# Two attention layers on one core: VectorE's exponential in five steps instead of seven, and eleven more tiles for it

## The chip, the core and the metric

The kernel runs on one core of one Trainium2 chip. The metric is the device time of one execution, in microseconds. Every run is listed with its time and with the mean clock that the profile shows as granted to TensorE, 1.000 being full speed. I call a run clean when its mean clock was 1.000. The experiments came in four sets, each on another chip with its own runs of the kernel before; the clean runs of that kernel have means of 1062.06 to 1062.43 us in the four sets, so comparisons across sets are good to some 0.4 us.

## The reference

Two equal layers over 2048 rows of 448, each an attention with 16 heads of 28 and an MLP with two gelus. Cut to what matters here:

```python
def _A_ref(x, wqkv, wo):
    qkv = (x @ wqkv).reshape(B, S, 3, H, Dh) ...          # S 2048, H 16, Dh 28
    scores = jnp.einsum("bhqd,bhkd->bhqk", q, k) * (Dh ** -0.5)
    p = _softmax(scores, axis=-1)                         # 16 x 2048 x 2048 exponentials per layer
    o = jnp.einsum("bhqk,bhkd->bhqd", p, v)
    return ... @ wo

x = A_x
x = x + _A_ref(_layernorm(x), A_wqkv, A_wo)
x = x + _B_ref(_layernorm(x), B_w1, B_w2, B_w3, B_w4)     # _B_ref: gelu(ln(x)@w1), shifts, @w2, gelu(ln@w3)@w4
x = x + _A_ref(_layernorm(x), A_wqkv, A_wo)
x = x + _B_ref(_layernorm(x), B_w1, B_w2, B_w3, B_w4)
```

## The kernel before

The 2 x 16 x 2048 x 2048 scores are 2048 tiles of 128x512. TensorE writes them into PSUM in 821 groups of alternately three and two tiles. ScalarE makes the exponentials of a group with one instruction. Some groups of three give their third tile to VectorE, where the program computes 2^x with integer arithmetic and a cubic in the fraction. `OFFL` says which groups these are.

```python
OFFL = ((48, 104, 6), (104, 150, 8), (150, 204, 6), (204, 300, 8), (500, 600, 8), (640, 731, 6))
EXPC = (0.30457565 * 128, 0.07826797 * 128)

def on_dve(n):                      # does group n give its third tile to VectorE?
    if len(grans[n]) < 3:
        return False
    ...
    return 1 <= grans[n][2][1] <= ... - 4 and any(a <= n < b and n % m == 0 for (a, b, m) in OFFL)

# VectorE's exponential (each yield op is one instruction; the buffer arguments are cut)
yield op("dve", ..., e.tensor_scalar(out=t32, in0=ps[:, bk, :], scalar1=0.0, scalar2=65536.0, op0=ALU.max, op1=ALU.mult))
yield op("dve", ..., e.tensor_scalar(out=fx, in0=lo, scalar1=2.0 ** -16, op0=ALU.mult))
yield op("dve", ..., e.tensor_scalar(out=ex, in0=fx, scalar1=EXPC[1], scalar2=EXPC[0], op0=ALU.mult, op1=ALU.add))
yield op("dve", ..., e.tensor_tensor(out=ex, in0=ex, in1=fx, op=ALU.mult))
yield op("dve", ..., e.tensor_scalar(out=fx, in0=fx, scalar1=-1.0, op0=ALU.add))
yield op("dve", ..., e.tensor_tensor(out=ex, in0=ex, in1=fx, op=ALU.mult))
yield op("dve", ..., e.scalar_tensor_tensor(out=PTD[:, slot, :], in0=t32, scalar=2.0 ** -9, in1=ex, op0=ALU.mult, op1=ALU.add))

# ScalarE's exponential of group n: cnt is 3, or 2 where VectorE has the third tile
yield op("act", e_dur(n), e.activation(out=PT[:, p0:p0 + cnt, :], in_=ps[:, b0:b0 + cnt, :], func=ACT.Exp, ...))
```

The order of all the instructions is not written by hand. When the program is built, a small scheduler plays the engines forward with estimated durations and picks what goes next. Where TensorE would wait, the scheduler adds a filler product of ones that nobody reads:

```python
SC.fill = (0.13, lambda e, b: e.matmul(out=ps[:, bi(b), 0:256], lhsT=ones_bf, rhs=ones_bf..., start=True, stop=True), ...)
```

The order was searched. `MOVES` holds two lists of (time, seed) pairs. At each time of the plan a random change, made from the seed, is applied to the latest starts by which the scheduler ranks its tasks. The lists are what a search over the scheduler's own estimate of the end has left:

```python
MOVES = [
    [(0.00, 453789), (24.05, 533123), (36.08, 574974), ...],      # 56 pairs
    [(0.00, 702263), (12.33, 381949), (24.47, 834893), ...],      # 56 pairs
]
plan = None
for k in range(ROUNDS):
    res = attempt(plan); plan = res[2].latest_starts(res[0])
for moves in MOVES[:-1]:
    res = attempt(plan, moves); plan = res[2].latest_starts(res[0])
est, P, SC = attempt(plan, MOVES[-1])
```

Of the kernel before, what the change touches and what calls it, by code (L numbers as in the profile page):

```python
# [8 lines left out]
ALU = mybir.AluOpType  # L9
# [487 lines left out]
def build_kernel(nc, A_x, A_wqkv, A_wo, B_x, B_w1, B_w2, B_w3, B_w4, out, n_layers=2):  # L497
# [11 lines left out]
    BIAS2 = 127.0  # L509
    WSH = 60.0 / LN2 + BIAS2  # L510
    DEFER = 4
    OFFL = ((48, 104, 6), (104, 150, 8), (150, 204, 6), (204, 300, 8), (500, 600, 8), (640, 731, 6))
    EXPC = (0.30457565 * 128, 0.07826797 * 128)
    TINY = 1e-20
    KCM = [(0, 112), (1, 112), (2, 112), (3, 112)]
    UBK = 5
    ROUNDS = 2
    MOVES = [
        [
            (0.00, 453789), (24.05, 533123), (36.08, 574974), (48.13, 374121), (60.22, 17501), (84.27, 918064), (96.41, 203548), (108.45, 909555),  # L520
            (120.45, 357456), (132.60, 615296), (168.83, 148562), (205.39, 389665), (229.56, 260273), (266.42, 71036), (278.44, 70253), (290.45, 97573),
            (314.58, 848798), (326.69, 359077), (338.81, 922778), (351.11, 731965), (364.52, 922857), (388.69, 388342), (400.73, 341387), (412.89, 278637),
            (425.04, 936161), (437.08, 80124), (449.22, 970104), (461.26, 151723), (473.36, 509392), (485.67, 278223), (497.71, 363728), (511.25, 320651),
            (523.31, 527451), (547.67, 931336), (572.39, 152194), (608.57, 394582), (620.75, 516554), (644.95, 174795), (669.10, 437522), (681.11, 304397),
            (693.35, 108309), (790.42, 21658), (838.85, 985952), (850.87, 674587), (862.89, 750586), (886.96, 618177), (929.37, 284043), (941.41, 596069),
            (953.46, 140073), (965.63, 696548), (977.66, 436165), (1001.89, 686219), (1014.11, 556019), (1026.13, 187601), (1038.16, 491035), (1050.33, 406353),
        ],
        [
            (0.00, 702263), (12.33, 381949), (24.47, 834893), (48.87, 33421), (61.01, 651789), (73.13, 100529), (85.19, 168019), (109.41, 146449),
            (146.15, 574177), (182.31, 891325), (194.40, 548019), (219.14, 396368), (231.29, 936970), (267.99, 701177), (280.01, 389568), (304.46, 941668),  # L530
            (316.78, 35337), (328.87, 201463), (353.05, 620046), (370.67, 421032), (382.82, 496206), (407.05, 974502), (419.21, 461357), (431.23, 484152),
            (443.42, 453671), (455.47, 313724), (479.69, 235889), (491.75, 227868), (516.71, 902926), (528.71, 143541), (540.72, 193750), (552.80, 710760),
            (576.97, 844584), (588.99, 232721), (601.11, 752264), (631.15, 288695), (643.22, 852623), (655.22, 951063), (679.25, 59294), (691.29, 109340),
            (703.74, 727887), (752.74, 761501), (777.12, 29398), (789.20, 616564), (801.25, 815928), (813.34, 33117), (837.60, 194148), (850.22, 728687),
            (890.63, 232155), (926.81, 41726), (939.16, 676561), (975.81, 264839), (987.86, 695881), (1003.27, 65585), (1027.57, 125777), (1039.58, 587050),
        ],
    ]
    GATE1 = ('qr', 0)
# [28 lines left out]
    def c_ps(n):  # L567
        return 0.07 + n * 0.00104

    def c_f2b(n):  # L570
        return 0.07 + n * 0.00052

    def c_b2b(n):
        return 0.07 + n * 0.00026
# [8 lines left out]
    with st:  # L583
        def sb(name, shape, dt):
            return st.enter_context(nc.sbuf_tensor(name, shape, dt))
# [6 lines left out]
        t32 = sb("t32", [128, 512], mybir.dt.int32)  # L592
# [15 lines left out]
        gt = sb("gt", [128, 512], FP32)  # L608
# [47 lines left out]
        def op(eng, dur, fn, reads=(), writes=(), **kw):  # L656
            return (eng, dur, fn, list(reads), list(writes), kw)
# [473 lines left out]
        def on_dve(n):  # L1131
            if len(grans[n]) < 3:
                return False
            L, u, g, p, kts, first, last = segs[grans[n][2][0]]
            return 1 <= grans[n][2][1] <= len(kts) * UNITS[L][u][1] // 4 - 4 and any(a <= n < b and n % m == 0 for (a, b, m) in OFFL)

# [15 lines left out]
        def pt_key(n, k):  # L1152
            return ("ptd", DVN[n]) if n in DVN and k == 2 else ("pt", n % 6)

        def t_dexp(n):
            bk, slot, at = gbank(n) + 2, DVN[n], DVL.index(n)
            yield ("acq", ["t32"])
            yield op("dve", 0.06 + c_ps(512), lambda e: e.tensor_scalar(out=t32[:, :], in0=ps[:, bk, :], scalar1=0.0, scalar2=65536.0, op0=ALU.max, op1=ALU.mult),  # L1158
                     reads=[("ps", bk)], writes=[("t32",)], last=[("ps", bk)])
            yield ("sig", ("d1", n))  # L1160
            for r in ("gt0", "gt1"):
                yield ("acq", [r])
            fx, ex = gt[:, 0:256].bitcast(FP16), gt[:, 256:512].bitcast(FP16)
            lo = t32[:, :].bitcast(mybir.dt.uint16).rearrange("p (n two) -> p n two", two=2)[:, :, 0]
            yield op("dve", c_f2b(512), lambda e: e.tensor_scalar(out=fx, in0=lo, scalar1=2.0 ** -16, scalar2=None, op0=ALU.mult), reads=[("t32",)], writes=[(("gt",), "gt0")])
            yield op("dve", c_b2b(512), lambda e: e.tensor_scalar(out=ex, in0=fx, scalar1=EXPC[1], scalar2=EXPC[0], op0=ALU.mult, op1=ALU.add),
                     reads=[(("gt",), "gt0")], writes=[(("gt",), "gt1")])
            yield op("dve", c_f2b(512), lambda e: e.tensor_tensor(out=ex, in0=ex, in1=fx, op=ALU.mult), reads=[(("gt",), "gt0"), (("gt",), "gt1")], writes=[(("gt",), "gt1")])
            yield op("dve", c_b2b(512), lambda e: e.tensor_scalar(out=fx, in0=fx, scalar1=-1.0, scalar2=None, op0=ALU.add), reads=[(("gt",), "gt0")], writes=[(("gt",), "gt0")])
            yield op("dve", c_f2b(512), lambda e: e.tensor_tensor(out=ex, in0=ex, in1=fx, op=ALU.mult), reads=[(("gt",), "gt0"), (("gt",), "gt1")], writes=[(("gt",), "gt1")])  # L1170
            if at >= 3:
                yield ("wait", ("pvd", DVL[at - 3]))
            yield op("dve", 0.06 + c_ps(512), lambda e: e.scalar_tensor_tensor(out=PTD[:, slot, :].bitcast(mybir.dt.uint16), in0=t32[:, :], scalar=2.0 ** -9, in1=ex, op0=ALU.mult, op1=ALU.add),
                     reads=[("t32",), (("gt",), "gt1")], writes=[pt_key(n, 2)])
            for r in ("gt0", "gt1", "t32"):
                yield ("rel", r)
            yield ("sig", ("d", n))

        def gbank(n):
            return 3 * (n % 2)  # L1180
# [35 lines left out]
        def t_attention():  # L1216
# [42 lines left out]
            for n in (0, 1):  # L1259
                if n in DVN:  # L1260
                    yield ("spawn", t_dexp(n), 1)
            for n in range(N):
                for (si, i, j) in grans[n]:
                    if i == 0 and j == 0:
                        yield ("sig", ("segstart", si))
                        if not segs[si][5]:
                            yield ("spawn", t_uload(si), 1)
                yield from pt_free(n)
                b0, p0, cnt = gbank(n), gblk(n), n_act(n)
                yield op("act", e_dur(n), lambda e, b0=b0, p0=p0, cnt=cnt: e.activation(out=PT[:, p0:p0 + cnt, :], in_=ps[:, b0:b0 + cnt, :], func=ACT.Exp, scale=LN2, bias=-BIAS2 * LN2),  # L1270
                         reads=[("ps", b0 + k) for k in range(cnt)], writes=[pt_key(n, 0)], tab="exp", main=n, last=[("ps", b0 + k) for k in range(cnt)])
                yield ("sig", ("e", n))
                if n + 2 < N:
                    yield from st_ops(n + 2)
                    if n + 2 in DVN:
                        yield ("spawn", t_dexp(n + 2), 1)
# [471 lines left out]
def bass_interleave_layers__mha_block__mixer_s_mlp__prompt_kernel(nc, A_x, A_wqkv, A_wo, B_x, B_w1, B_w2, B_w3, B_w4, out):  # L1748
    build_kernel(nc, A_x, A_wqkv, A_wo, B_x, B_w1, B_w2, B_w3, B_w4, out)
# [28 lines left out]
```

## Time and profile before

| | before |
|---|---|
| median of the first three runs | 1062.92 us (1061.68 to 1065.45) |
| its 42 runs beside the experiments | mean 1063.47 us, mean clock 0.9985 |
| 13 of these, the clean ones | mean 1062.24 us |
| profiled run | 1062.14 us, clock 1.0 |
| tiles on VectorE | 39 |
| ScalarE busy, TensorE busy, VectorE busy | 1022.6, 1022.5, 708.1 us |

How to read it: a page lists per engine its busy time and its share of the span, and then rows in which the span is cut into 40 slices with a digit for the busy tenths of each. The lines that bound the kernel are shown in the prediction below. One row of that page was left out there. It is TensorE's granted clock in tenths, slice by slice (a 9 is 90% or more):

```profile
PEclk9999999999999999999999999999999999999999
```

In the profiled run the clock never fell (1.00 in all stretches).

### The profile page before, as it was taken

The page shows a single profiled execution, that of the slowest core. Times are in us where ns is not written, and L with a number is a line of the kernel's source. Part 1 is how long each engine was busy: PE and PEld are TensorE (multiplying, and loading weights), DVE is VectorE, ACT ScalarE, POOL GpSimd, SP SyncE. Part 2 cuts the span into 40 slices and gives each one's busy share as a digit, 9 for nine tenths or more (in the row PEclk, how much of TensorE's full clock was granted, in tenths as well). Part 3 has the DMA queues.
Part 4 walks back from the last instruction along what each step waited for, and adds up shares of the span by engine and source line. Part 5 has one row for each costly group of instructions (what it writes and reads, how often), then busy time and mean ns, then how long its engine had stood idle before and what let it go on. Part 6 is the DMA issues. An engine that isn't in the chain of part 4 may idle for free.

```text
span 1060.3 us, 20859 instructions
## 1 busy us (share of the span) xinstructions
PE 1022.5 (96%) x8896; PEld 397.1 (37%) x8912; DVE 708.1 (67%) x1707; ACT 1022.6 (96%) x939; POOL 56.9 (5%) x78
## 2 busy tenths in 40 slices
PE   8999999999999999999999999999999999999998
PEld 5233333333333333334333443333333333444446
DVE  7977678775877647863489426657777966377544
ACT  6999999999999999999999999999999999999984
POOL 2000000000001001010010000000010100010000
PEclk9999999999999999999999999999999999999999
DMA  4232140000010001100020002211120001010000
GB/s 116 81 108 83 36 121 21 16 1 21 3 19 21 1 1 40 36 21 1 1 61 31 27 11 61 70 32 48 32 45 1 2 21 35 23 25 2 1 19 23
DMA packets 70709, 35.01 MB, mean 33 GB/s; under 512 B 56472, under 2 KB 65048, under 8 KB 70616
## 3 DMA queue, kind: packets, MB, share of 16 engines
q1 hardware_dynamic: 70616, 33.68, 11.9%
q8 instruction: 69, 1.13, 0.4%
q14 instruction: 24, 0.20, 0.1%
HBM read 12.70 MB, written 7.08 MB: 19 GB/s over the span
## 4 chain that ended last, share of the span: by engine, by line
ACT 60%; PE 34%; DVE 4%; DMA 1%; issue 1%; POOL 0%; SPq 0%; POOLq 0%; DVEq 0%
ACT PT L1270 53%; PE ps L661 9%; PE ps L1244 9%; PE ps L1319 8%; PE ps L1687 5%; ACT h2T L1651 4%; PE ps L664 3%; ACT L1651 1%; ACT gt L1434 1%; ACT L1270 1%; DMA h2T<-in_A_wqkv_dram 1%; DVE hT L1407 1%; DVE qT L969 0%; DMA uscr<-uin 0%; DVE gw L1420 0%
## 5 line engine op out<-in xcount | busy, mean ns | idle before, releaser
L1270 ACT ACTIVATE PT<-ps 128x1024 bf16<-128x1024 f32 (+1 forms) x821 | 921.7, 1227 | 5.5 <-PE ps L1244 2.5
L1244 PE MATMUL ps<-qT,kT 32*128 32x512 bf16 (+1 forms) x2304 | 320.7, 360 | 13.0 <-ACT PT L1270 8.0
L1319 PE MATMUL ps<-PT,vaug 128*32 128x512 bf16 (+1 forms) x2264 | 249.7, 361 | 4.7 <-ACT PT L1270 2.6
L1244 PEld LDWEIGHTS ps<-qT,kT 32*128 32x128 bf16 x2304 | 80.6, 91 | 257.6 <-ACT PT L1270 136.2
L1687 PE MATMUL ps<-ones_bf 128*128 128x256 bf16 x1001 | 155.1, 279 | 2.7 <-DVE hot L695 1.1
L661 PE MATMUL ps<-xT,w 112*128 112x512 bf16 (+6 forms) x618 | 128.8, 324 | 1.5 <-DVE h2T L1610 0.5
L1610 DVE CAST h2T<-ps 128x512 bf16<-128x512 f32 (+2 forms) x126 | 73.7, 585 | 79.8 <-PE ps L661 68.8
L1687 PEld LDWEIGHTS ps<-ones_bf 128*128 128x128 bf16 x1001 | 83.1, 99 | 76.0 <-issue 57.2
L1319 PEld LDWEIGHTS ps<-PT,vaug 128*32 128x32 bf16 x2264 | 64.6, 94 | 123.4 <-issue 66.1
L661 PE MATMUL ps<-w,h2T 128*128 128x448 bf16 x388 | 89.4, 354 | 3.4 <-ACT h2T L1651 2.4
L661 PEld LDWEIGHTS ps<-xT,w 112*128 112x128 bf16 (+1 forms) x618 | 50.0, 104 | 52.9 <-issue 25.5
L664 PE MATMUL ps<-xT,w 112*32 112x512 bf16 (+3 forms) x632 | 51.5, 343 | 0.3 <-DVE hT L1407 0.2
L1158 DVE TENSOR_SCALAR t<-ps 128x512 int32<-128x512 f32 x39 | 26.8, 687 | 35.3 <-PE ps L1244 35.3
L661 PEld LDWEIGHTS ps<-w,h2T 128*128 128x128 bf16 x388 | 33.0, 97 | 40.5 <-issue 14.1
L1651 ACT ACTIVATE h2T<-h2T 128x7168 bf16<-128x7168 bf16 (+2 forms) x9 | 44.8, 5010 | 0.1
L1569 POOL TENSOR_TENSOR mst<-mst,neghalf 128x1 f32<-128x1 f32 x32 | 24.4, 772 | 346.2 <-DVE mst L1567 346.1
L824 DVE BATCH_NORM_STATS2 st<-x_res 128x6 f32<-128x448 bf16 x64 | 39.1, 614 | 1.5 <-DMA x_res<-in_A_x_dram 1.0
L1634 DVE TENSOR_TENSOR x_res<-x_res,ps 128x448 bf16<-128x448 bf16 x16 | 9.9, 619 | 44.7 <-PE ps L661 40.8
L1341 DVE STREAM_TRANSPOSE u_sb<-ps 128x512 f32<-128x512 f32 (+1 forms) x24 | 15.0, 625 | 33.5 <-PE ps L1319 33.2
L1627 DVE TENSOR_TENSOR uin<-x_res,ps 128x448 bf16<-128x448 bf16 x16 | 9.9, 618 | 32.3 <-PE ps L661 23.2
L933 DVE TENSOR_SCALAR kT<-ps,cols 128x512 bf16<-128x512 f32 (+3 forms) x36 | 22.5, 628 | 12.3 <-PE ps L661 8.6
L1348 DVE SCALAR_TENSOR_TENSOR uin<-uin,fct,ps 128x512 f32<-128x512 f32 x20 | 14.8, 742 | 23.6 <-PE ps L1319 22.7
(144 smaller groups left out, 1029.3 us busy)
## 6 DMA issues: line engine op xcount, KB each, us to landing
uin<-uscr SPq DMA_DIRECT2D x20, 256.0 KB, 2.6
uscr<-u_sb SPq DMA_DIRECT2D x12, 256.0 KB, 2.0
uscr<-uin SPq DMA_DIRECT2D x8, 256.0 KB, 2.1
out_dram<-uin SPq DMA_DIRECT2D x16, 112.0 KB, 1.7
w<-in_B_w_dram SPq DMA_DIRECT2D x4, 392.0 KB, 4.2
x_res<-in_A_x_dram SPq DMA_DIRECT2D x3, 448.0 KB, 8.6
w<-in_B_w_dram SPq DMA_DIRECT2D x2, 448.0 KB, 6.5
h2T<-in_A_wqkv_dram SPq DMA_DIRECT2D x2, 392.0 KB, 5.6
```

The source lines that it names most:

```text
L661: return e.matmul(out=dst(0, m), lhsT=lhs(0, m), rhs=rhs, start=start, stop=stop)
L664: return [e.matmul(out=dst(a, min(m, a + 32)), lhsT=lhs(a, min(m, a + 32)), rhs=rhs, start=start, stop=stop, tile_position=(0, a)) for a i ...
L824: yield op("dve", 0.55, lambda e: e.bn_stats(out=st6[:, t, :], in_=x_res[:, t, :]), reads=[("x", t)], writes=[("st6", t)])
L933: yield op("dve", 0.06 + c_ps(nw), lambda e, b=b: e.tensor_scalar(out=dst, in0=ps[:, bi(b), 0:nw], scalar1=mul, scalar2=bias, op0=ALU.mult ...
L1158: yield op("dve", 0.06 + c_ps(512), lambda e: e.tensor_scalar(out=t32[:, :], in0=ps[:, bk, :], scalar1=0.0, scalar2=65536.0, op0=ALU.max, ...
L1244: yield op("pe", 0.005 if ph == h else 0.012 + W / 2400.0, lambda e, bk=bk, r0=32 * j, g=g, kc=kc, q0=q0, W=W, c0=W * h: e.matmul(out=ps[: ...
L1270: yield op("act", e_dur(n), lambda e, b0=b0, p0=p0, cnt=cnt: e.activation(out=PT[:, p0:p0 + cnt, :], in_=ps[:, b0:b0 + cnt, :], func=ACT.E ...
L1319: yield op("pe", nt * 0.054 if item in late else 0.004 + nt * 0.0133, lambda e, j=j, rhs=rhs, vs=vs, i=i: e.matmul(out=ps[32 * j:32 * j + ...
L1569: yield op("pool", 0.57, lambda e, t=t: e.tensor_tensor(out=mst[:, t, R3:R3 + 1], in0=mst[:, t, V3E:V3E + 1], in1=neghalf[:, 0:1], op=ALU. ...
L1610: yield op("dve", c_ps(NW), lambda e, fch=fch, b=b: e.tensor_copy(out=h2T[:, fch, hoff:hoff + NW], in_=ps[:, bi(b), 0:NW]), reads=[("ps", ...
L1651: yield op("act", c_act(14 * NW), lambda e, c0=c0, NW=NW: e.activation(out=h2T[:, :, c0:c0 + NW], in_=h2T[:, :, c0:c0 + NW], func=ACT.Gelu ...
L1687: SC.fill = (0.13, lambda e, b: e.matmul(out=ps[:, bi(b), 0:256], lhsT=ones_bf[:, :], rhs=ones_bf[:, :].unsqueeze(1).to_broadcast([128, 2, ...
```

## The change

The intent: ScalarE bounds the kernel, VectorE has room. So make VectorE's exponential shorter and give it more tiles, among them some where layer 1 ends and layer 2 begins, which had none. The cubic 128 f (f - 1)(0.0783 f + 0.3046) is kept. With a = (0.0783 x 128)^(1/3) and g = a f it becomes g (g - a)(g + b), which two fused instructions compute. The seeds come from a new search for the new load.

```diff
-    OFFL = ((48, 104, 6), (104, 150, 8), (150, 204, 6), (204, 300, 8), (500, 600, 8), (640, 731, 6))
-    EXPC = (0.30457565 * 128, 0.07826797 * 128)
+    OFFL = ((48, 104, 6), (104, 300, 6), (372, 411, 6), (480, 520, 6), (520, 600, 8), (640, 731, 6))
+    EXPA = (0.07826797 * 128) ** (1 / 3)
+    EXPB = EXPA * 0.30457565 / 0.07826797
 ...
     MOVES = [
         [
-            (0.00, 453789), (24.05, 533123), ...                  # cut: 56 pairs
+            (0.00, 453789), (32.56, 797911), ...                  # cut: 39 pairs
         ],
         [
-            (0.00, 702263), (12.33, 381949), ...                  # cut: 56 pairs
+            (0.00, 951844), (12.28, 444188), ...                  # cut: 69 pairs
         ],
     ]
 ...                                                               # buffer arguments cut
-            yield op("dve", c_f2b(512), ... e.tensor_scalar(out=fx, in0=lo, scalar1=2.0 ** -16, op0=ALU.mult))
-            yield op("dve", c_b2b(512), ... e.tensor_scalar(out=ex, in0=fx, scalar1=EXPC[1], scalar2=EXPC[0], op0=ALU.mult, op1=ALU.add))
-            yield op("dve", c_f2b(512), ... e.tensor_tensor(out=ex, in0=ex, in1=fx, op=ALU.mult))
-            yield op("dve", c_b2b(512), ... e.tensor_scalar(out=fx, in0=fx, scalar1=-1.0, op0=ALU.add))
-            yield op("dve", c_f2b(512), ... e.tensor_tensor(out=ex, in0=ex, in1=fx, op=ALU.mult))
+            yield op("dve", c_f2b(512), ... e.tensor_scalar(out=fx, in0=lo, scalar1=EXPA * 2.0 ** -16, op0=ALU.mult))
+            yield op("dve", c_ps(512), ... e.scalar_tensor_tensor(out=ex, in0=fx, scalar=-EXPA, in1=fx, op0=ALU.add, op1=ALU.mult))
+            yield op("dve", c_ps(512), ... e.scalar_tensor_tensor(out=ex, in0=fx, scalar=EXPB, in1=ex, op0=ALU.add, op1=ALU.mult))
```

## The prediction

What is left to price the fused instruction is an estimate: the trace before has no `scalar_tensor_tensor` with 16-bit operands alone, and the 689 ns are those of L1173, which has a 32-bit input. The rival is that a fused instruction takes 424 ns, as the `tensor_tensor` of L1168 and L1170 does. The 0.2 us for a lone value product are an estimate too. In the trace before, four value products start between 192.709 and 192.719 us, each of 389 or 390 ns; of the 40 that read a VectorE tile, 15 start with no other product within 12 ns.

> **What bounds the kernel now.** I read the page first (busy time, then the 40 slices, then the chain that ended last), then ScalarE's and VectorE's groups with shapes kept apart, then the busy time by stretches, last the waits of ScalarE alone. The page:
>
> ```profile
> PE 1022.5 (96%) x8896; PEld 397.1 (37%) x8912; DVE 708.1 (67%) x1707; ACT 1022.6 (96%) x939; POOL 56.9 (5%) x78
> ...
> DVE  7977678775877647863489426657777966377544
> ACT  6999999999999999999999999999999999999984
> ...
> ACT PT L1270 53%; PE ps L661 9%; PE ps L1244 9%; PE ps L1319 8%; PE ps L1687 5%; ACT h2T L1651 4%; PE ps L664 3%; ACT L1651 1%; ACT gt L1434 1%; ACT L1270 1%; DMA h2T<-in_A_wqkv_dram 1%; DVE hT L1407 1%; DVE qT L969 0%; DMA uscr<-uin 0%; DVE gw L1420 0%
> ```
>
> Two engines are at 96%, so the busy shares alone don't name the bound. TensorE is padded: 155.1 us of its time are filler products of ones (L1687), put in where it would have waited. ScalarE has no such padding. The softmax exponentials (L1270) head the chain with 53%. The TensorE pieces in it are mostly work just in time between two exponentials, as the next view shows. It gives the busy time before the first exponential, from there to the end of the last batched gelu at 1028 us, and after:
>
> ```profile
> 0.00:26.90 26.90, 23.39 (x166) 13.96 (x168) 19.77 (x82) 16.94 (x25) 6.88 (x18) 1.00 0.43 114
> 26.90:1028.00 1001.10, 970.00 (x8462) 363.86 (x8476) 673.52 (x1590) 993.39 (x878) 45.40 (x55) 1.00 0.12 31
> 1028.00:1060.40 32.40, 29.10 (x270) 19.33 (x270) 14.86 (x37) 12.25 (x38) 4.59 (x7) 1.00 0.06 19
> ```
>
> The columns are PE, PEld, DVE, ACT, POOL. In the 1001.1 us of the middle ScalarE is idle for 1001.10 - 993.39 = 7.7 us, under 1%. So the time is: 27 us of start, ScalarE's sum in the middle plus its 7.7 us of gaps, and 32 us of tail. A microsecond taken off ScalarE in the middle is a microsecond of the end, as long as no new gap opens. What its remaining waits are, from its own waits:
>
> ```profile
> ACT PT L1270 <- PE ps L1244: 2.5, 11, 0.4
> ACT gt L1434 <- DVE gw L1423: 1.9, 4, 0.7
> ACT PT L1270 <- PE ps L1319: 0.8, 2, 0.6
> ACT qT L931 <- PE ps L661: 0.3, 1, 0.3
> ```
>
> No wait is over 0.7 us, and the exponentials hardly ever wait for VectorE: the seven-step exponential is off the path.
>
> **The rows that price the change.** Groups of ScalarE and VectorE by shape:
>
> ```profile
> L1270 ACT ACTIVATE PT<-ps 128x1536 bf16<-128x1536 f32 x370 | 540.8, 1461 | 2.8 <-PE ps L1244 1.4
> L1270 ACT ACTIVATE PT<-ps 128x1024 bf16<-128x1024 f32 x448 | 456.7, 1037 | 2.7 <-PE ps L1244 1.1 <-PE ps L1319 0.8
> ...
> L1173 DVE SCALAR_TENSOR_TENSOR PTD<-t,gt 128x512 uint16<-128x512 int32 x39 | 26.9, 689 | 1.0
> L1158 DVE TENSOR_SCALAR t<-ps 128x512 int32<-128x512 f32 x39 | 26.8, 687 | 35.3 <-PE ps L1244 35.3
> ...
> L1170 DVE TENSOR_TENSOR gt<-gt 128x512 f16<-128x512 f16 x39 | 16.5, 424 | 1.1
> L1168 DVE TENSOR_TENSOR gt<-gt 128x512 f16<-128x512 f16 x39 | 16.5, 424 | 1.1
> L1165 DVE TENSOR_SCALAR gt<-t 128x512 f16<-128x512 uint16 x39 | 16.4, 421 | 0.7
> ...
> L1169 DVE TENSOR_SCALAR gt<-gt 128x512 f16<-128x512 f16 x39 | 11.4, 292 | 1.1
> L1166 DVE TENSOR_SCALAR gt<-gt 128x512 f16<-128x512 f16 x39 | 11.3, 290 | 1.0
> ```
>
> The 2048 score tiles of 128x512 go in 821 groups of alternately three and two. Where the plan gives a group's third tile to VectorE, ScalarE's instruction is 1024 wide in place of 1536: that is what one offloaded tile is worth, 1461 - 1037 = 424 ns.
>
> [...]
>
> **The change part by part.**
>
> *Five steps for seven.* The polynomial 128 f (f - 1)(0.0783 f + 0.3046) is kept; a factor EXPA on f and a shift EXPB let two fused instructions do what two `tensor_scalar` and two `tensor_tensor` did. Removed: 290 + 424 + 292 + 424 = 1430 ns. Added: two `scalar_tensor_tensor` [...]2 x 689 = 1378 ns. The tile was 687 + 421 + 1430 + 689 = 3227 ns and becomes 687 + 421 + 1378 + 689 = 3175 ns: 52 ns or 1.6%, and two gaps of some 0.03 us (1.1 us of idle over 39). So I hold the fusion for almost worthless by itself[...]. It leaves ScalarE untouched. For the 39 tiles that existed it gives VectorE back 39 x 0.052 = 2.0 us.
>
> *More tiles.* I evaluated the plan's rule over all 821 groups: a group of three, its number divisible by the range's last figure, its third tile neither in the first row of its segment nor among the last three. Before 39 tiles qualify, after 50. Groups 104 to 149: 5 to 6. 150 to 203: 7 and 7. 204 to 299: 10 to 12. 372 to 410: none to 5. 480 to 599: 3 to 6. 48 to 103 and 640 on: unchanged with 4 and 10. Sum +1 +2 +5 +3 = +11. ScalarE loses 11 x 0.424 = 4.66 us. Its 1536-wide count falls to 359, its 1024-wide count rises to 459.
>
> *VectorE pays* 50 x 3.175 - 39 x 3.227 = 158.8 - 125.9 = +32.9 us, to 741 us, about 70% of the span. The average hides where it lands. By counting exponentials, groups 372 to 410 run at about 450 to 498 us and 480 to 519 at about 580 to 622 us, each just ahead of a gelu batch. The stretches of those (columns as above):
>
> ```profile
> 450.00:498.00 48.00, 47.31 (x370) 16.14 (x370) 27.65 (x70) 48.00 (x43) 2.68 (x4) 1.00 0.05 12
> ...
> 578.00:624.00 46.00, 45.51 (x409) 18.36 (x408) 22.44 (x54) 45.97 (x42) 2.32 (x3) 1.00 0.08 23
> ```
>
> VectorE has 48.00 - 27.65 = 20.4 us free in the first, and five tiles need 5 x 3.175 = 15.9 us: it fits, tightly, to 43.5 of 48. In the second 23.6 us are free for 4 tiles, 12.7 us. What lies there otherwise is the copying of layer products out of PSUM (L1610), which gates TensorE's MLP products and the gelu batch; late copies would only move that batch by a few exponentials, since ScalarE goes on with others meanwhile.
>
> *TensorE.* An offloaded tile's value product runs alone rather than in a set of four on separate columns. A lone one adds perhaps 0.2 us of TensorE (my estimate, about half of the 390 ns that one such matmul lasts): 11 x 0.2 = 2 us, out of 155 us of filler. In the two new stretches the filler is 6.3 and 2.9 us, so it is thin but not gone.
>
> *The new order.* The diff also replaces the two lists of seeds that perturb the order of instructions. It does not add work. It can move ScalarE's 7.7 us of gaps, and start and tail by a microsecond or so, either way. The order has been fitted to the heavier load, so I put the gaps at 7.5 to 8.5 us, +0.2 in the middle.
>
> Sum: 1062.9 - 4.7 + 0.2 = 1058.4 us, 0.4% less.
>
> **The rivals.**
>
> *VectorE becomes the bound locally.* For it: at 440 to 460 us it is busy 19.4 of 20 us, and at 560 to 580 19.7 of 20, next to the new tiles. Against it: the new ranges begin after these peaks, the bank of an offloaded tile is freed by the first of the five steps, and ScalarE's waits on VectorE are 1.9 us today. If each of the 11 tiles cost a wait of 0.4 us, the gain would be gone: 1063 us. Badly placed tiles, with 1 us each, would give 1069 us.
>
> *TensorE becomes the bound where the tiles were added.* The exponentials of 450 to 498 us get 5 x 0.424 = 2.1 us shorter, so scores must come faster while filler is thin. If all eight tiles of the two stretches (5 + 3) gain nothing, only 3 x 0.424 = 1.3 us remains: 1061.7 us.
>
> [...]With all operands 16-bit it may take 424 ns like the `tensor_tensor`. The tile would then be 2.65 us and VectorE 50 x 2.65 - 125.9 = +6.6 us. The end would hardly change, as VectorE isn't on the path: 1058 us still, with less risk.
>
> *The new order finds more.* If the search removed half of the 7.7 us of gaps and a microsecond of the tail, 1053.5 us.
>
> **Range and chances.** The three runs before spread by 3.8 us, and the middle of three is good to perhaps 1 us (my estimate). Below, the better order and a lucky run reach 1054; above, both bound rivals reach 1062. I take 1054.0 to 1062.0. A 2% change is 21 us: a gain so large would need over four times the work that leaves ScalarE, a loss 2 us for every added tile. Faster 0.01, same 0.98, slower 0.01.
>
> **What would show it.** 1536-wide exponentials 359 and 1024-wide 459, and ScalarE busy near 1018 us: the arithmetic of the tiles. Two fused rows with 50 each at about 689 ns[...]; about 424 ns would refute it. VectorE near 741 us. ScalarE's idle in the middle 7 to 9 us: no new wait. Wrong would be new idle ahead of L1270 put down to TensorE or VectorE at 450 to 500 or 580 to 622 us, or a tail longer than 33 us; then the gain is smaller than the tiles' sum. If the time falls by more than 7 us, the new order did it, not the tiles.

## The result, and the profile after

The changed kernel took 1066.13 us in the median of six runs (1064.70 to 1069.07), the kernel before 1063.51 us in six (1061.68 to 1065.45). The ratio is 1.0025, 95% interval 1.0005 to 1.0045: within 2%, as expected, but above the range, and in the other direction. A ratio here and below is taken over the fast runs of the same rounds, so it is not quite the ratio of the quoted medians.

The page of the changed kernel, its busy times and TensorE's clock:

```profile
PE 1031.8 (97%) x9485; PEld 396.7 (37%) x9485; DVE 745.9 (70%) x1683; ACT 1018.8 (96%) x940; POOL 58.0 (5%) x78
...
PEclk8999999999999999999989999999999999999999
```

ScalarE's busy time fell by 3.8 us and VectorE's rose to 746 us, close to what was predicted. The clock row shows two slices with an 8 that were 9s before. Next, ScalarE's and VectorE's groups by shape (busy us, mean ns of one, then the idle time just before them and what ended it):

```profile
L1269 ACT ACTIVATE PT<-ps 128x1536 bf16<-128x1536 f32 x359 | 527.0, 1468 | 8.2 <-PE ps L1243 4.3 <-PE ps L1318 2.0
L1269 ACT ACTIVATE PT<-ps 128x1024 bf16<-128x1024 f32 x459 | 468.5, 1044 | 3.5 <-PE ps L1243 2.9
...
L1167 DVE SCALAR_TENSOR_TENSOR gt<-gt 128x512 f16<-128x512 f16 x50 | 34.5, 691 | 1.3
...
L1168 DVE SCALAR_TENSOR_TENSOR gt<-gt 128x512 f16<-128x512 f16 x50 | 34.4, 688 | 1.3
```

The counts are the predicted 359 and 459, and the fused instructions take 688 and 691 ns. But the exponentials now sit idle for 8.2 + 3.5 = 11.7 us, where it was 2.8 + 2.7 = 5.5 us, and they wait for TensorE's scores (L1243) and value products (L1318). The busy times by stretch, cut as the prediction cut them (columns PE, PEld, DVE, ACT, POOL, then the clock):

```profile
0.00:30.20 30.20, 26.30 (x171) 14.30 (x171) 20.10 (x84) 17.47 (x27) 5.19 (x14) 0.89 0.38 101
30.20:1032.50 1002.30, 976.09 (x9034) 362.57 (x9033) 710.17 (x1562) 989.55 (x877) 48.48 (x58) 0.99 0.13 31
1032.50:1065.80 33.30, 29.41 (x281) 19.84 (x281) 15.65 (x39) 11.79 (x37) 4.29 (x7) 1.00 0.07 22
```

The start is 30.2 instead of 26.9 us, ScalarE is idle in the middle for 1002.30 - 989.55 = 12.8 us instead of 7.7, and the tail is 33.3 instead of 32.4 us. So each of the three parts took something back. And ScalarE's longest single source of waits, the one that was 2.5 us in 11 waits before:

```profile
ACT PT L1269 <- PE ps L1243: 7.2, 16, 1.3
```

Asked for by window, 5.0 of these 7.2 us lie between 545 and 580 us, mostly at half clock, in groups 440 to 446. The longest wait for a value product (1.8 us) is at 906 us. In the stretches where tiles were added about the middle (groups 372 to 410 at 465 to 506 us and 480 to 519 at 602 to 655 us by the starts of the exponentials) ScalarE has no wait at all; up to 450 us, where the other added tiles are, the waits for scores are 1.5 us, against 1.6 in the kernel before.

The clock's part shows in short stretches. After (three stretches of 5 us):

```profile
10.00:15.00 5.00, 2.76 (x47) 1.84 (x45) 2.94 (x6) 4.02 (x7) 0.00 (x0) 0.95 0.58 200
...
545.00:550.00 5.00, 4.14 (x49) 1.80 (x47) 5.00 (x20) 4.83 (x6) 0.00 (x0) 1.00 0.16 57
550.00:555.00 5.00, 5.00 (x32) 2.08 (x31) 3.49 (x10) 3.06 (x3) 0.00 (x0) 0.54 0.46 105
```

And before:

```profile
10.00:15.00 5.00, 3.82 (x38) 2.73 (x39) 3.25 (x13) 4.73 (x7) 0.12 (x1) 1.00 0.63 216
...
545.00:550.00 5.00, 4.25 (x43) 1.52 (x43) 3.53 (x8) 5.00 (x5) 0.00 (x0) 1.00 0.52 127
550.00:555.00 5.00, 4.95 (x44) 2.04 (x44) 3.94 (x10) 5.00 (x6) 0.00 (x0) 1.00 0.01 3
```

In the changed kernel TensorE has little to do from 10 to 15 us (2.76 us of 5, 3.82 before), and then runs at half clock for 6.8 us. At 550 us it runs at half clock for 10.2 us; TensorE is then busy all the time with 32 products in 5 us where the kernel before runs 44, and ScalarE, which waits for them, is busy for 3.06 us of 5. The trace has only two values of the clock in these places, 1.0 and 0.5.

The halvings whose length can be given came as 3.41 us (after_fill_start at 14.2 us, before_again at 567 us), 6.83 us (the changed kernel at 14.5 us, before_thin_start at 11.8 us) and 10.24 us (the changed kernel at 550 us): one, two and three times 3.41. Idle time of TensorE alone doesn't account for them: in the 3.41 us before the halving at 14.5 us it had been busy for 1.95 us, and in those before the one at 550 us for 2.69 us (4.14 us of the 5 us in the row above).

Of the six runs of the changed kernel none was clean: their mean clocks are 0.990, 0.992, 0.992, 0.995, 0.995 and 0.996. Of the 42 runs of the kernel before that were made beside the experiments below (mean 1063.47 us, mean clock 0.9985), 13 were clean (mean 1062.24 us), 27 had 0.998, one 0.997 and one 0.995. Time goes with clock: a straight line through these 42 runs gives 1062.2 us at full clock and 0.83 us for each 0.001 of mean clock.

### The profile page after: what moved, and what is told of

The parts are those of the page before. It is cut to its first block, busy times and chain, and to the rows that moved or that the text cites. A ratio compares the mean times of both kernels' runs of the same rounds, so it can differ in the third digit from the quotient of the medians.

```text
span 1065.8 us, 21991 instructions
## 1 busy us (share of the span) xinstructions
PE 1031.8 (97%) x9485; PEld 396.7 (37%) x9485; DVE 745.9 (70%) x1683; ACT 1018.8 (96%) x940; POOL 58.0 (5%) x78
## 3 DMA queue, kind: packets, MB, share of 16 engines
q1 hardware_dynamic: 70616, 33.68, 12.8%
## 4 chain that ended last, share of the span: by engine, by line
ACT 54%; PE 40%; DVE 4%; DMA 1%; issue 0%; SPq 0%; POOL 0%; POOLq 0%; DVEq 0%; ACTq 0%
ACT PT L1269 47%; PE ps L662 12%; PE ps L1243 11%; PE ps L1318 9%; PE ps L1686 5%; ACT h2T L1650 4%; PE ps L665 3%; ACT L1650 1%; ACT gt L1433 1%; DMA xT<-xn 1%; ACT L1269 1%; DMA h2T<-in_A_wqkv_dram 1%; DVE hT L1406 0%; PE ps L872 0%; DVE xn L896 0%
## 5 line engine op out<-in xcount | busy, mean ns | idle before, releaser
L1269 ACT ACTIVATE PT<-ps 128x1024 bf16<-128x1024 f32 (+1 forms) x821 | 918.2, 1228 | 11.7 <-PE ps L1243 7.2
L1243 PE MATMUL ps<-qT,kT 32*128 32x512 bf16 (+1 forms) x2304 | 322.3, 361 | 13.4 <-ACT PT L1269 11.4
L1318 PE MATMUL ps<-PT,vaug 128*32 128x512 bf16 (+1 forms) x2253 | 268.1, 363 | 3.3 <-ACT PT L1269 2.2
L1243 PEld LDWEIGHTS ps<-qT,kT 32*128 32x128 bf16 x2304 | 80.7, 91 | 263.4 <-ACT PT L1269 160.4
L1686 PE MATMUL ps<-ones_bf 128*128 128x256 bf16 x893 | 138.6, 278 | 1.8 <-DVE hot L696 1.1
L1318 PEld LDWEIGHTS ps<-PT,vaug 128*32 128x32 bf16 x2253 | 67.6, 94 | 135.6 <-issue 83.0
L662 PE MATMUL ps<-xT,w 112*128 112x512 bf16 (+6 forms) x574 | 115.6, 320 | 1.2 <-DVE h2T L1609 0.4
L1686 PEld LDWEIGHTS ps<-ones_bf 128*128 128x128 bf16 x893 | 73.2, 99 | 67.4 <-issue 49.3
L665 PE MATMUL ps<-xT,w 112*32 112x512 bf16 (+3 forms) x808 | 71.9, 350 | 0.3 <-DVE qT L970 0.2
L662 PE MATMUL ps<-w,h2T 128*128 128x448 bf16 x257 | 61.2, 354 | 0.4 <-ACT h2T L1606 0.4
L1159 DVE TENSOR_SCALAR t<-ps 128x512 int32<-128x512 f32 x50 | 34.3, 686 | 32.5 <-PE ps L1243 32.1
L665 PE MATMUL ps<-w,h2T 128*32 128x448 bf16 x764 | 49.4, 353 | 3.8 <-ACT h2T L1650 2.4
L1167 DVE SCALAR_TENSOR_TENSOR gt<-gt 128x512 f16<-128x512 f16 x50 | 34.5, 691 | 1.3
L1172 DVE SCALAR_TENSOR_TENSOR PTD<-t,gt 128x512 uint16<-128x512 int32 x50 | 34.5, 689 | 1.3
L1168 DVE SCALAR_TENSOR_TENSOR gt<-gt 128x512 f16<-128x512 f16 x50 | 34.4, 688 | 1.3
```

The costliest lines, as they stand in the source:

```text
L662: return e.matmul(out=dst(0, m), lhsT=lhs(0, m), rhs=rhs, start=start, stop=stop)
L665: return [e.matmul(out=dst(a, min(m, a + 32)), lhsT=lhs(a, min(m, a + 32)), rhs=rhs, start=start, stop=stop, tile_position=(0, a)) for a i ...
L1167: yield op("dve", c_ps(512), lambda e: e.scalar_tensor_tensor(out=ex, in0=fx, scalar=-EXPA, in1=fx, op0=ALU.add, op1=ALU.mult), reads=[((" ...
L1168: yield op("dve", c_ps(512), lambda e: e.scalar_tensor_tensor(out=ex, in0=fx, scalar=EXPB, in1=ex, op0=ALU.add, op1=ALU.mult), reads=[(("g ...
L1172: yield op("dve", 0.06 + c_ps(512), lambda e: e.scalar_tensor_tensor(out=PTD[:, slot, :].bitcast(mybir.dt.uint16), in0=t32[:, :], scalar=2 ...
L1243: yield op("pe", 0.005 if ph == h else 0.012 + W / 2400.0, lambda e, bk=bk, r0=32 * j, g=g, kc=kc, q0=q0, W=W, c0=W * h: e.matmul(out=ps[: ...
```

## The experiments

Theory A, formed after reading the two traces: the tiles bring what was predicted or a little less, the fusion nothing; the new order gives part of it back at full clock, in the start, the tail and new waits; and it leaves TensorE thin in two places, so that its clock halves more often. Theory B: the added tiles themselves cost waits, because VectorE and TensorE have no room for them where they were put. Theory C: the fusion hurts, as VectorE's steps came later. Thirteen kernels ran, all with correct results; each set shared its runs of the kernel before.

**A control.** The kernel before once more, unchanged.

> The kernel before, unchanged, as a control: ratio 1.000, and it shows the TensorE clock of each of its runs, which was not listed so far. The clock theory (the kernel after is slower because its thinner TensorE work lets the clock halve for stretches of 7 to 10 us) expects mean clocks of 0.999 to 1.000 in most of these runs, against 0.990 to 0.996 in the six runs after, and that the slower of them (1065 us) are the ones with a lower clock. If clocks of 0.992 are as common here, the clock does not tell the two kernels apart.

Measured: 1063.13 us median, ratio 0.9993 (0.9980 to 1.0006). In its profiled run the clock halved once, for 3.41 us at 567 us. So the method finds no difference where there is none, to about 0.13% either way, and the kernel before has halvings too, but short ones.

**The fusion alone.** The order of the kernel before is kept instruction by instruction; the two instructions that fall away leave empty places in the plan.

```diff
-  tensor_scalar(ex, fx, EXPC[1], EXPC[0], mult, add); tensor_tensor(ex, ex, fx, mult)
-  tensor_scalar(fx, fx, -1.0, add);                   tensor_tensor(ex, ex, fx, mult)
+  (empty place); scalar_tensor_tensor(ex, fx, -EXPA, fx, add, mult)
+  (empty place); scalar_tensor_tensor(ex, fx, EXPB, ex, add, mult)
```

> The kernel before with its instruction order frozen: the five-step exponential put into the slots of the seven-step one, two instructions dropped, the same 39 tiles. All theories: VectorE busy 2 us less, the end unchanged, ratio 0.999 to 1.001. If the fused instructions delay the value products, groups would wait more and it would be slower than 1.001.

Measured: 1063.13 us, ratio 0.9998 (0.9985 to 1.0012). The fused instructions took 688 ns each. Its three clean runs have a mean of 1062.86 us, 0.6 us above those of the kernel before, which themselves spread over more than that (1061.3 to 1063.1 us). So no effect of the fusion is seen, to about 0.15% either way, and theory C falls as an account of the loss.

**The clock alone.** Extra filler products are added to the changed kernel where its TensorE is thin: in the plan's 10.6 to 14 us after every third product and in groups 434 to 442 after every fourth; then in the start only; then lighter, every second product at the start and every sixth in groups 436 to 439.

```diff
+    GUARD = (("t", 10.6, 14.0, 3), ("main", 434, 443, 4))    # after_fill_both
+    GUARD = (("t", 10.6, 14.0, 3),)                          # after_fill_start
+    GUARD = (("t", 10.6, 14.0, 2), ("main", 436, 440, 6))    # after_fill_light
```

> The kernel after in its own order, with extra filler products on TensorE in the two thin stretches: between the tiny column sums at 10 to 14 us, and in groups 434 to 442, which run at about 541 to 551 us. Clock theory: no halving at 14 and 550 us, first exponential at 27 us instead of 30.2, some 5 us less waiting in groups 425 to 449; time 1066.1 - 3.3 - 5.0 = 1058 us, ratio to before about 0.995. Load theory (VectorE or TensorE is too full with 50 tiles, or the new order is worse as such): extra products do nothing good, 1066 us or more, ratio 1.0025 or above.

Measured: 1064.07 us, ratio 1.0018 (0.9998 to 1.0037). Four of six runs were clean, at 1063.63 to 1064.07 us; the other two had 0.994 and took 1068.5 us. So the filling took away most of the halvings, and still the clean runs are not faster than those of the kernel before. The clock is only part of the loss.

> The same with the extra products at 10 to 14 us alone. Clock theory: the start's halving goes (3.3 us), the one at 550 us stays; 1062 to 1063 us, ratio about 0.9995, mean clock 0.995. Load theory: as after, 1066 us.

Measured: 1066.03 us, ratio 1.0024 (0.9999 to 1.0049). Filling the start alone did not prevent the halving there (one of 3.41 us at 14.2 us in the profiled run, with TensorE busy for 3.44 us of the 5 from 10 us on). One run happened to be clean: 1061.53 us, the only clean run near the changed kernel's own order. A straight line through these six runs and the six of the changed kernel gives 1061.6 us at full clock and 0.76 us for each 0.001.

> The kernel after in its own order, with denser extra products at 10 to 14 us and fewer in the middle (groups 436 to 439, after every sixth product instead of every fourth in 434 to 442). Clock theory: mean clock near 1.000 in most runs, and without the load of the heavier filling 1061.5 to 1062.5 us, ratio 0.9975 to 0.9985: the kernel after at full clock. Not 1058: the start that is 1.7 us later, the tail that is 1 us longer and waits in groups 625 to 724 belong to the new order and stay.

Measured: 1063.23 us, ratio 1.0014 (0.9994 to 1.0033). Four clean runs at 1062.45 to 1063.24 us, mean 1062.95; two others had 0.993 and 0.994. If the 1061.6 us of the line are right (the fit's own standard error is 0.3 us), the filling itself costs something: 2.3 us in after_fill_both (clean mean 1063.94) and 1.3 us here. These costs are estimates; no run shows the filling alone.

The profiled run of after_fill_both has a clock of 1.00 throughout, as that of the kernel before has. So these two can be compared part by part without the clock in it. Cut at the start of the first exponential and the end of the last, after_fill_both:

```profile
0.00:28.60 28.60, 25.23 (x184) 14.82 (x185) 19.98 (x84) 17.47 (x27) 5.19 (x14) 1.00 0.40 107
28.60:1024.50 995.90, 966.81 (x8949) 360.92 (x8963) 705.75 (x1552) 984.92 (x875) 48.31 (x57) 1.00 0.12 31
1024.50:1062.35 37.85, 33.45 (x367) 22.67 (x363) 19.49 (x48) 16.26 (x39) 4.50 (x7) 1.00 0.07 23
```

And the kernel before, cut the same way:

```profile
0.00:26.86 26.86, 23.35 (x166) 13.96 (x168) 19.73 (x82) 16.90 (x24) 6.84 (x18) 1.00 0.43 114
26.86:1023.44 996.58, 966.53 (x8398) 362.32 (x8411) 669.89 (x1580) 988.96 (x876) 45.40 (x54) 1.00 0.12 31
1023.44:1060.25 36.81, 32.60 (x334) 20.87 (x333) 18.53 (x46) 16.72 (x41) 4.63 (x7) 1.00 0.06 20
```

ScalarE's busy time in the middle falls by 988.96 - 984.92 = 4.04 us, and that is what the tiles take off it. Its idle time there goes from 7.62 to 10.98 us, which takes back 3.36 us. The start takes 1.74 us more and the tail 1.04 us. The sum is -4.04 + 3.36 + 1.74 + 1.04 = +2.10 us, the difference of the two spans. Of the waits, 3.3 us for scores lie between 530 and 565 us, where the kernel before has none and where fillers were added, and 1.8 us for a value product at 903 us, where none were. So some of the 3.36 us may be the filling's own cost; the tail's part is not, as the changed kernel's tail is 37.84 us without it. In the start the new order has TensorE make sixteen q products before the first scores, where the old one makes twelve; that is the trace's order of things, and I tested no kernel that changes only that.

**Does half a clock cost as much at the start?** The kernel before, with the fillers of the plan's 9 to 14.5 us left out, so that its clock halves there.

```diff
+    THIN = ((9.0, 14.5),)       # no filler product is added in this stretch of the plan
```

> The converse: the kernel before, order frozen, with only the filler products between 9 and 14.5 us of its plan left out. Clock theory: the clock halves at about 14 us in every run, as in the kernel after; first exponential at 29 to 30 us instead of 26.7, 2 to 3 us slower, ratio 1.002 to 1.003, mean clock 0.996 to 0.997. If the filler has no part in it: 1063.5 us as before.

Measured: 1063.81 us, ratio 1.0008 (0.9996 to 1.0020), no clean run among five (0.997 four times, 0.995 once). The busy times of its profiled run, 10 to 15 us:

```profile
10.00:15.00 5.00, 1.55 (x14) 1.06 (x15) 2.27 (x8) 4.77 (x7) 0.00 (x0) 0.68 0.62 214
```

So in this stretch fillers kept the clock up: without them (1.55 us of TensorE in 5 us, 3.82 with them) it halved for 6.83 us, and the first exponential came at 28.7 us instead of 26.9 us (26.7 in before_again). The mean is 0.7 us above that of all runs of the kernel before and 1.9 us above its clean ones. A halving is real and costs about 1 to 2 us when it is that short; it doesn't make the whole difference.

**The tiles alone.** Eleven tiles are added to the order of the kernel before (with five steps), which otherwise stays as it is, but for which of three buffers a VectorE tile is put into: groups 80, 236, 292, 376, 392, 400, 414, 480, 490, 496 and 506.

```diff
+    EXTRA = (80, 236, 292, 376, 392, 400, 414, 480, 490, 496, 506,)
+        P = add_tiles(P)        # moves their third tile to VectorE, their value product four rows later
```

> The order of the kernel before, frozen, with five steps and 11 more tiles moved to VectorE (groups 80, 236, 292, 376, 392, 400, 414, 480, 490, 496, 506: where VectorE was idle long enough), nothing else moved: 50 tiles, as in the kernel after, without the new order. If the tiles are worth what was predicted and the new order lost it: 11 x 0.427 = 4.7 us less than the kernel before at the same clock, about 1058.5 to 1059.5 us, ratio 0.9955 to 0.9965. If the load of 50 tiles on VectorE or their lone value products on TensorE ate the gain: 1062 to 1066 us, ratio 0.999 or more.

The 0.427 us, here and in two later expectations, are the estimate in the program's own scheduler (`e_dur`). The trace before has 1461 - 1037 = 424 ns.

Measured: 1068.30 us, ratio 1.0052 (1.0037 to 1.0067). The one clean run took 1066.42 us: 4.2 us more than the kernel before, where eleven tiles should have brought 4.7 us less. In its profiled run ScalarE's waits for scores rose from 2.5 us in 11 waits to 11.5 us in 24. By the distances between the exponentials' starts the delay sits just behind the added tiles: 1.5 us at group 395, 1.2 at 404, 1.1 at 493, 1.4 at 499. That run was not clean, though: it took 1069.01 us, with halvings at 503 and 571 us. A wait of 1.5 us at 575 us follows the second of them and is in before_five_steps too, so not all of the 9.0 us of new waits are the tiles' doing. The loss of 4.2 us rests on one clean run, and the next kernel's clean run bears it out. In an order that was not planned for it, a tile taken from ScalarE can be worth less than nothing. This is what theory B says, but it is shown for the old order only.

> The same with extra filler products on TensorE in the two stretches where the kernel before lets its clock halve in some runs (9 to 18 us, and groups 451 to 455 at about 564 us). Clock theory: mean clock 1.000 in most runs, 1 us less than without: 1057 to 1058.5 us. If the extra products hold up the scores more than the clock gives back: the same as without, or 1 us more, at a clock of 1.000.

Measured: 1069.60 us, ratio 1.0064 (1.0050 to 1.0078), clean run 1067.43 us. It is the same kernel with more filler in its start and in groups 451 to 455. That did not help, so these 4 us are not the clock.

**The tiles in the new order.** In after_fill_light some of VectorE's tiles are given back to ScalarE, with nothing else changing its place: eleven of them, then thirty-five.

```diff
+    RETURN = (132, 138, 222, 234, 246, 270, 294, 372, 390, 396, 492,)
+        P = give_back(P)
```

> The converse of adding tiles to the order of before: the kernel after with the light filling, its order frozen, and 11 of its 50 tiles (groups 132, 138, 222, 234, 246, 270, 294, 372, 390, 396, 492) given back to ScalarE. If a tile is worth its 0.427 us of ScalarE in an order that was planned for it: the stretch from the first to the last exponential grows by 11 x 0.427 = 4.7 us, and the time from 1063.0 us (light filling, full clock) to 1067.7 us, ratio 1.004. If TensorE is as much a bound as ScalarE, so that waits take the place of what a tile saves: less than half of it, under 1065 us.

Measured: 1067.75 us, ratio 1.0053 (1.0030 to 1.0075). Three clean runs at 1066.18 to 1066.44 us, mean 1066.28: 3.33 us over the clean runs of after_fill_light, or 0.30 us for each tile. One other run had a mean clock of 0.946 and took 1073.44 us; it is left out of this.

> The same with 35 tiles given back, for the slope: 35 x 0.427 = 14.9 us more, 1078 us, ratio 1.014, if tiles are worth their ScalarE time; under 1070 us if waits for TensorE take their place.

Measured: 1074.87 us, ratio 1.0118 (1.0100 to 1.0135). Three clean runs, mean 1074.75 us: 11.8 us over after_fill_light, or 0.34 us for each tile. So in the new order the tiles do bring most of their time: 3.3 to 3.7 us for eleven, of 4.7 predicted. Theory B falls for the changed kernel. The other side of the same number: with 39 tiles, the new order and the light filling take 1066.3 us clean, against 1062.2 us of the old order with as many tiles. Less the 1.3 us of the filling, the new order by itself costs nearly 3 us. This is an estimate: the 39 tiles are not the same ones, and the order was searched for 50. The start and tail above, 1.74 + 1.04 = 2.8 us later at full clock, are of the same size.

**The seeds alone.** The changed kernel with its 50 tiles and five steps, but with the two lists of seeds of the kernel before.

```diff
-    MOVES = [[(0.00, 453789), (32.56, 797911), ...], [(0.00, 951844), (12.28, 444188), ...]]
+    MOVES = [[(0.00, 453789), (24.05, 533123), ...], [(0.00, 702263), (12.33, 381949), ...]]
```

> The changed kernel with its tiles and its five steps, but with the two lists of seeds of the kernel before. Theory, the lists fit only the tile plan that they were searched for, and order is worth far more than the tiles: this is slower than both kernels by several per cent (the program's own estimate of the end is 56 us higher), ratio 1.03 to 1.06, the loss being idle time of ScalarE spread over many groups. Rival, as the prediction had it, that the lists only move gaps by a microsecond or so: 1060 to 1066 us, ratio 0.998 to 1.004.

Measured: 1117.44 us, ratio 1.0522 (1.0480 to 1.0564). The exponentials in its profile:

```profile
L1269 ACT ACTIVATE PT<-ps 128x1536 bf16<-128x1536 f32 x359 | 523.8, 1459 | 43.2 <-PE ps L1243 37.4 <-PE ps L1318 4.0
L1269 ACT ACTIVATE PT<-ps 128x1024 bf16<-128x1024 f32 x459 | 464.4, 1034 | 12.6 <-PE ps L1243 11.6 <-PE ps L1318 0.5
```

The same work, the same counts, and 55.8 us of idle time before the exponentials instead of 11.7, 49.0 us of it waiting for scores. At these tiles the two pairs of lists lie 51 us apart, eleven times what the tiles were to bring. They fit only the load for which they were searched. Its start is the shortest of all, by the way (first exponential at 22.2 us), and its middle 1051 us.

**Towards a better kernel.** Two attempts. One keeps the old order and adds only five tiles, each at a place where a replay of the trace's durations showed room. The other keeps the 50 tiles and the light filling and takes a third list of seeds, from a further search whose estimate of the end is 0.55 us lower.

```diff
+    EXTRA = ((300, 4, 0), (374, 4, 0), (402, 4, 0), (480, 4, 0), (508, 4, 0), )   # before_5_tiles, on before_five_steps
```

> The order of the kernel before, kept instruction by instruction, with the exponential in five steps and five more tiles for VectorE (groups 300, 374, 402, 480 and 508), chosen one by one because neither TensorE nor VectorE is short of time right there. Theory: a tile is worth its 0.3 to 0.4 us only where its neighbours leave room for it, so five well placed tiles bring 1.5 to 2 us, while eleven at the places of the changed plan cost 4 us: at full clock 1060.3 to 1060.9 us against 1062.3 of the kernel before, ratio near 0.998. Start and tail stay those of the kernel before (first exponential near 26.7 us, tail near 36.8 us). Rival, any tile added to an order that was not planned for it opens waits that eat it: 1062.3 to 1064 us, ratio 1.000 to 1.002.

Measured: 1063.14 us, ratio 0.9999 (0.9986 to 1.0013). Its two clean runs took 1061.12 and 1061.91 us, 0.7 us less than the mean clean run of the kernel before; its other three had 0.997 and 0.998. The five tiles took 1.6 us off ScalarE's busy time in the profiled run, so less than half of that is left (1.3 us against the clean runs of before_five_steps, from which only the tiles differ; with two and three runs the one figure is no better than the other), and over all runs, halvings included, nothing that could be shown.

```diff
-            (0.00, 951844), (12.28, 444188), (24.31, 919282), ...
+            (0.00, 951844), (11.76, 605641), (12.28, 444188), (24.31, 919282), ...   # after_best, on after_fill_light
```

> The changed kernel with the light filling of the start and of the groups 436 to 439, and with another list of seeds for the order, found by a further search over the program's own estimate of the end, which says 0.55 us less than for the changed kernel's list. Theory, the estimate carries over to the chip to about half a microsecond and nothing else moves: 1062.4 us at full clock, against 1062.95 of the same filling with the list of the change and 1062.3 of the kernel before; with its usual halvings the ratio to the kernel before is 1.000 to 1.002. Rival, the order decides more than the estimate sees (start, tail, halvings): anything from 1061 to 1065 us at full clock, and new halvings elsewhere.

Measured: 1062.60 us, ratio 0.9995 (0.9982 to 1.0008), four of five runs clean, mean of these 1062.35 us. It has the lowest median of all kernels here, and that median is 0.3% below the changed kernel's, which was measured in other rounds. But its interval against the kernel before holds 1. No version is shown to beat the kernel before. These two can't be told from it, within some 0.15%.

The profiled runs side by side, from the busy times by stretch (us; the middle runs from the first exponential's start to the last one's end; the changed kernel's row includes two halvings and that of after_old_seeds three; the others have none):

| profiled run | start | middle | of it ScalarE busy | idle | tail | end |
|---|---|---|---|---|---|---|
| before | 26.86 | 996.58 | 988.96 | 7.62 | 36.81 | 1060.25 |
| before_5_tiles | 27.26 | 995.33 | 987.37 | 7.96 | 36.81 | 1059.40 |
| after | 30.20 | 997.76 | 985.08 | 12.68 | 37.84 | 1065.80 |
| after_fill_both | 28.60 | 995.90 | 984.92 | 10.98 | 37.85 | 1062.35 |
| after_best | 28.65 | 993.79 | 984.64 | 9.15 | 37.51 | 1059.95 |
| after_old_seeds | 22.22 | 1050.95 | 988.31 | 62.64 | 39.51 | 1112.68 |

## Why the prediction was right or wrong

*The bound and the counts: right.* ScalarE still bounds the middle. The counts 359 and 459, ScalarE at 1018.8 us (predicted near 1018) and VectorE at 745.9 us (predicted 741) came out. VectorE is 5 us over; the fused rows alone would not do that, and I did not look for the rest, as no wait of weight on VectorE came of it. One reading was wrong: by the starts of the exponentials, groups 372 to 410 run at 463 to 515 us in the kernel before and groups 480 to 519 at 598 to 653 us, each with a gelu batch inside it, not at 450 to 498 and 580 to 622 us ahead of one. VectorE has more free time there (36.0 and 33.8 us) than the 20.4 and 23.6 us that were counted, so the conclusion that the tiles fit stands.

*Five steps for seven: right.* The estimate of 689 ns, taken from L1173, held: 688 and 691 ns. The rival with 424 ns is refuted. That the fusion is almost worthless by itself is shown by before_five_steps, ratio 0.9998.

*Eleven tiles at 0.424 us: mechanism right, size too large.* By the two give-back kernels a tile is worth 0.30 to 0.34 us, so 3.3 to 3.7 us of the 4.66. Where the rest goes was not traced, as the profiled runs of both give-back kernels had a lowered clock.

*Both bound rivals: not what happened here.* They feared new waits where tiles were added, and the sign named was new idle time ahead of the exponentials at 450 to 500 or 580 to 622 us. There is none there, nor in the stretches where those groups really run. The waits for scores did grow, 7.2 us instead of 2.5, but between 545 and 580 us, in groups of the range 411 to 479, of which VectorE has no tile. VectorE itself is named by 0.8 us of waits. The tail of 33.3 us is just over the 33 us that were named as a sign. "Each tile costs a wait" is what happened in the old order (before_11_tiles, 4.2 us lost), which was not planned for the tiles.

*The new order: this is the step that failed.* The prediction said that the diff's new seeds "can move ScalarE's 7.7 us of gaps, and start and tail by a microsecond or so, either way", and took "7.5 to 8.5 us, +0.2 in the middle". At 50 tiles the two pairs of seed lists lie 51 us apart (after_old_seeds), so what a list of seeds does isn't a matter of a microsecond or so. With 12.8 us of gaps in the changed kernel and 11.0 us where the clock was full (after_fill_both), with a start 1.7 us longer at full clock and a tail 1.0 us longer, the order gave back about 3 us at equal clock, where +0.2 was put down.

*The second failure was something left out.* The prediction read 1.00 in the clock column of each stretch before and kept it for after, though it counted 155 us of filler. Filler went down to 893 products and 138.6 us from 155.1, and it lay elsewhere. The changed kernel's clock was 0.993 in the mean of its six runs. By the slope of 0.76 us for each 0.001 that is 5 us. The 42 runs of the kernel before have 0.9985, which is 1.2 us by their slope of 0.83. So some 4 us of the loss are the clock's, if the lines hold.

The sum as the runs give it, each term an estimate from the means above: the fusion 0; eleven tiles -3.3 to -3.7; the new order at full clock about +3, so that the two kernels would be within 1 us at full clock (1061.6 by the line, 1062.2 measured); and the clock +4. Together some +3.4 us. Measured in the same rounds, mean against mean: 1066.39 - 1063.70 = +2.7 us. The full-clock value of the changed kernel is the weakest number in this: it is drawn from a line and from one clean run of its sibling, as the kernel itself was never seen clean in six runs. If the light filling cost nothing, that value would be the 1062.95 us of after_fill_light, the order would have cost 4 us and the clock 2, and the sum would come out as well. That both took part is shown; how they share the loss is not.

*Open.* Why the first scores come later in the new order was read from the trace and not tested. What makes the clock halve in one run and not in another at the same place isn't settled either: with 3.44 us of TensorE work from 10 to 15 us it halved at 14 us in after_fill_start's profiled run, with 3.65 us it didn't in after_fill_both's, and with 2.97 us it didn't in before_11_tiles'. Nor does the share of busy time settle it: in the 3.41 us before a halving TensorE was busy for 57% (the changed kernel, at 14.5 us) and 79% (at 550 us), while in the kernel before it was busy for only 45% of such a stretch (1.55 us, up to 505.8 us) and the clock stayed at 1.00. These runs give no threshold.

## What to carry to other kernels

When the order of instructions comes from a search, a change of load and a new order are two changes, and the second can be the larger: try the load change in the old order and undo it in the new one before a gain is put down to either. Eleven tiles taken off the bounding engine lost 4.2 us in one order, and eleven (not quite the same) were worth 3.3 to 3.7 us in another; price a tile at what giving tiles back costs, not at the instruction's length. Read the granted clock of every run, not only that of the profiled one, and compare clean runs with clean runs: here the clock moved the time by 2 to 4 us, as much as the tiles did. And look where the new waits lie before they are put down to the change: here they were not where the tiles had been added.

## What else these runs show

- The fused `scalar_tensor_tensor` took 688 and 691 ns for 512 columns of f16, the same as the 689 ns of L1173 with a 32-bit input. Two of them save 51 ns over the two `tensor_scalar` (290 and 292 ns) and two `tensor_tensor` (424 ns each) that they replace: fewer instructions were worth next to nothing here, as the removed ones were the shorter ones.
- What a lowered clock cost this kernel, with ScalarE bounding its middle, was 0.76 to 0.83 us of time for each 0.001 of mean clock over 1065 us. The one run at a mean clock of 0.946 (1073.44 us) stays unexplained.
- In the kernel before, the shortest distance between the starts of two exponentials was 0.904 us for 1024 columns with a mean duration of 1037 ns, and 1.330 us for 1536 with 1461 ns, so an overlap of about 130 ns. ScalarE's idle time of 7.7 us is therefore not all the room there is: between consecutive exponentials of that kernel, the starts lay some 23 us in all further apart than these shortest distances.
- Leaving filler products out for 5.5 us of the plan brought a halving (before_thin_start, no clean run in five), and adding them cost an estimated 2.3 us (after_fill_both) or 1.3 us (after_fill_light).
